# One last routing group of eight units, both limited experts fixed after 16 units, and another seam between a Mamba-2 scan and a switch layer

## The chip, the cores and the metric

The kernel runs on one core of a Trainium2 chip. A core has five engines with a queue of instructions each: PE (TensorE, matmuls), ACT (ScalarE), DVE (VectorE), POOL (GpSimd) and SP (SyncE, which here only issues DMAs). They run side by side and wait for each other through semaphores; within a queue the order is that of the program. The metric is device time in microseconds (us) of one execution.

## The reference, cut to what matters

Two blocks follow each other. The first is a Mamba-2 scan over 4 sequences of 768 tokens with 8 heads of 32 elements and a state of 16; it is computed in chunks, with a masked product inside a chunk and a carried state between chunks. The second is a top-1 mixture of experts: each of the 3072 tokens picks one of 8 experts, is multiplied by two matrices with a Relu between, and is scaled by its gate.

```python
M = CB * L                                     # (C B^T) times decays, causal, within a chunk
y_intra = np.einsum('bhij,bhjd->bhid', M, xc)
y_inter = np.einsum('bhin,bhnd->bhid', Cc, state) * decay_to_i[:, :, :, None]
y[:, :, sl] = y_intra + y_inter
state = decay_full[:, :, None, None] * state + np.sum(Bx, axis=2)
...
logits = x @ w_gate                            # x is y with the heads side by side: (3072, 256)
expert_idx = np.argmax(logits, axis=1)
for e in range(E):
    mask = expert_idx == e
    xe = x[mask]
    h = np.maximum(xe @ w1[e], 0.0)
    ye = h @ w2[e]
    out[mask] = gate_w[mask, None] * ye
```

## The kernel before, in words

**Attention.** A unit is 128 tokens of one sequence; there are 24 units, numbered by chunk and then by sequence. The main loop has 12 steps `d`, each with the two units 2d and 2d+1. The order of instructions is written out by hand (`manual_schedule`), so what stands first in the source stands first in each engine's queue. A step holds, on PE: `rows` of the step before (L343, turns y back so that tokens lie on partitions, with the gate logits as extra columns), `own` (L287, this step's own contribution to the state), `y_old` (L322, the part from the carried state), in some steps `rank`, then `y_own` (L330, 16 matmuls with the masked product M), then `scores` of the next step (L273). DVE masks the scores (`weigh`, L278, one operation per unit), takes the rows out of PSUM (`rows_out`, L352) and sums the logits (L362). ACT copies y out of PSUM (`turned`, L336), makes the new state (`state`, L307) and masked copies of C (L261). POOL scales x (`scaled_x`, L266), adds the faded old state (L313) and writes finished rows to their places in HBM (`place`, L412).

**Routing.** Units form groups (`RGS`). When a group's logits are there, `choose` marks each token's expert and `count` adds up the group. One step later `rank` works out on PE at which place of its expert each token goes, `ranked` takes that out (L401, L402), and `place` stores a unit's 128 rows with one indirect DMA from POOL to the buffer `x_hbm`. Each expert has a first part of 256 places (P1) and a second one of up to 192 (P2). Experts 0 and 1 are limited: after a given number of units `cut` moves the next free place up to 256, so that the first part is fixed and can be read before the last tokens are ranked. Places left empty were filled beforehand with rows that point to no token. Expert 0 is limited after 16 units, expert 1 after 20. Because a place may write anywhere in `x_hbm`, it waits for reads of `x_hbm` that stand before it, and a read waits for the places before it.

**Seam.** After step 11 the attention's PSUM banks are given to the experts: four banks H for the up-projection (where g was), two banks Y for the output projection (where y was). The rows of step 11 are turned, expert 0's rows (tile `xs`, token by token) are transposed by PE (L518) and copied by ACT (L519), and the last four units are chosen.

**Experts.** For each expert, `m_h` makes 8 slices of 128 hidden elements: two matmuls of PE (L557) and a Relu on ACT (L566) per slice. `m_y` makes the output (L592), scaled by the gate (L579) and stored by an indirect DMA of POOL (L570). `between(f)` is called after slice `f` and issues what else is due: ranking and placing of the last group, reads (`m_load`), loads of weights, and the transposes of the next expert's rows (`m_xT`: tile `xb`, read with 256-byte pieces so that DVE can transpose it in blocks of 32, L526) with its gates. The second parts run at the end, in pairs of experts, at a size rounded up to a multiple of 4 from 128 on (`SIZES`).

Of the kernel before, what the change touches and what calls it, by code (L numbers as in the profile page):

```python
# [20 lines left out]
CH = 128  # L21
# [5 lines left out]
RGS = [4, 4, 4, 4, 4, 4]  # L27
CUT = 4
# [19 lines left out]
def ssd_then_moe(ctx, tc, xs_in, ae_in, wgx, w_gate, w1, w2, gx, gb, gc, ga, out):  # L48
# [233 lines left out]
    def own(d):  # L282
        if d // NP == NC - 1:
            return
        for s in range(2):
            for q in range(4):
                nc.tensor.matmul(A_ps[32 * q:32 * q + 32, 64 * s:64 * s + 64],  # L287
                                 lhsT=st[2 * d + s]["B"][:, 32 * q:32 * q + 32],
                                 rhs=st[2 * d + s]["xp"][:, 64 * q:64 * q + 64], start=(s == 0), stop=True,
                                 skip_group_check=True)  # L290
# [42 lines left out]
    def turned(d, a=0, b=KT):  # L333
        if a == 0:
            sd[d]["yT"] = wk.tile([128, KT, 2 * CH], FP32, name="yT")
        nc.scalar.copy(out=sd[d]["yT"][:, a:b], in_=y_ps[:, a:b, 0:2 * CH])  # L336
# [4 lines left out]
    def rows(d):  # L341
        for t, s in [(t, s) for t in range(KT) for s in range(2)]:
            nc.tensor.matmul(r_ps[:, s, 256 * t:256 * t + 160], lhsT=sd[d]["yT"][:, t, CH * s:CH * s + CH],  # L343
                                 rhs=turn[:, t].rearrange("p e h -> p (e h)"), start=True, stop=True,
                                 skip_group_check=True)

    def rows_out(d):
        n = 2 * d
        g = grp[n]
        k = n - R0[g]  # L350
        for a, b, o in ((0, D, 0), (D, DE, DM)):
            nc.vector.tensor_tensor(  # L352
                out=rt[g][:, k:k + 2, o:o + KT * 4 * (b - a)].rearrange("p s (t e h) -> p s t e h", t=KT, h=4),
                in0=r_ps.rearrange("p s (t z) -> p s t z", t=KT)[:, :, :, 4 * a:4 * b].rearrange(
                    "p s t (e h) -> p s t e h", h=4),
                in1=bc(Er[:, n:n + 2].rearrange("p s (t h) -> p s t h", h=4)[:, :, :, None, :],
                       [128, 2, KT, b - a, 4]), op=ALU.mult)
# [62 lines left out]
    def counts(g):  # L420
        p = r_ps[:, 1, 460:460 + E]
        nc.tensor.matmul(p, lhsT=ones_bf, rhs=cnt[:, g], start=True, stop=True, skip_group_check=True)
        return p

    def cut(e):


        p = r_ps[:, 1, 460:460 + E]
        c = cnt[0:1, CUT + e, e:e + 1]
        nc.vector.tensor_scalar(out=less[:, e:e + 1], in0=p[0:1, e:e + 1], scalar1=-float(P1), scalar2=0.0, op0=ALU.add,  # L430
                                op1=ALU.min)
        nc.vector.tensor_tensor(out=c, in0=c, in1=less[:, e:e + 1], op=ALU.subtract)
        if e == 0:
            nc.vector.tensor_reduce(bad[:, 0:1], p[0:1, 0:2], axis=AX, op=ALU.min)

    def over():
        p = r_ps[:, 1, 460:460 + E + 1]
# [30 lines left out]
    def m_load(i):  # L468


        p, e = jobs[i]
        if i == 0:
            xs = mo.tile([128, 2, W], FP32, name="xs")
            nc.sync.dma_start(out=xs, in_=x_hbm[e * NR:e * NR + P1, :].rearrange("(t p) w -> p t w", p=128))
            ex[i]["xs"] = xs
            ex[i]["lt"] = xs[:, :, DM:W]
            return
        r0, n = e * NR + P1 * p, (P1, P2)[p]
        xb = mo.tile([128, P1 // 32 * 64], FP32, name="xb", bufs=4)
        for c in range(4):  # L480
            nc.sync.dma_start(out=xb[32 * c:32 * c + 32, 0:2 * n].rearrange("p (r z) -> p r z", z=64),
                              in_=x_hbm[r0:r0 + n, 64 * c:64 * c + 64].rearrange("(r j) z -> j r z", j=32))
        ex[i]["xb"] = xb[:, 0:2 * n].rearrange("p (r i k) -> p k r i", k=KT, i=32)
        lt = mo.tile([128, 2, MID], FP32, name="lt", bufs=7)[:, 0:2 - p]
        nc.sync.dma_start(out=lt, in_=x_hbm[r0:r0 + 128 * (2 - p), DM:W].rearrange("(t p) w -> p t w", p=128))
        ex[i]["lt"] = lt
        if p and e % 2 == 0:
            lh = mo.tile([128, 1, MID], FP32, name="lh", bufs=3)
            for u in range(2):
                q = r0 + u * NR + 128  # L490
                nc.sync.dma_start(out=lh[64 * u:64 * u + 64, 0], in_=x_hbm[q:q + 64, DM:W])
            ex[i]["lh"] = ex[i + 1]["lh"] = lh
# [18 lines left out]
    def m_xT0():  # L511

        ex[0]["xT"] = mo.tile([128, KT, P1], FP32, name="xT", bufs=4)
        for k in range(KT):
            q = h_next()[:, 0:P1]
            for t in range(2):
                xs = ex[0]["xs"][:, t, 0:DM].rearrange("p (i k) -> p i k", k=KT)
                nc.tensor.transpose(q[:, 128 * t:128 * t + 128], xs[:, :, k], ident)  # L518
            nc.scalar.copy(ex[0]["xT"][:, k], q)  # L519

    def m_xT(i):
# [5 lines left out]
        for j in range(i, i + 1 + p):  # L527
            ex[j]["g"] = gates(ex[j]["lt"], 2 - p)
        if p:
            ex[i]["gh"] = gates(ex[i]["lh"], 1)  # L530
# [187 lines left out]
    with tc.manual_schedule():  # L718
# [37 lines left out]
        for d in range(ND):  # L756
# [23 lines left out]
            if k >= 0:  # L780
                rows(k)
            own(d)
# [6 lines left out]
            e_cut = {9: 0, 11: 1}.get(d)  # L789
            if q is not None:  # L790
                rank(q)
                if e_cut is not None:
                    counts(CUT + e_cut)
# [5 lines left out]
            if d < ND - 1:  # L799
                for s in range(2):  # L800
                    y_own(d, s, range(NH))
                if d == 4:
                    turn_both(1)
                turned(d)
                if d == 4:
                    take_both(1)
            else:
                for t in range(KT):
                    for s in range(2):
                        y_own(d, s, range(4 * t, 4 * t + 4))  # L810
                for t in range(KT):
                    turned(d, t, t + 1)
# [4 lines left out]
            if q is not None:  # L817
                ranked(q)
                if e_cut is not None:
                    cut(e_cut)  # L820
                todo += list(range(R0[q], R0[q] + RGS[q]))
            if k >= 0:
                rows_out(k)
                if d == 4:
                    take_totals(1)
            if d == 0:
                route_consts()
            if k >= 0:
# [18 lines left out]
            if d == 11:  # L847
                weakest()
        att.close()
# [5 lines left out]
        while todo:  # L855
            place(todo.pop(0))
        for k in range(4):
            load_w(1, 1, k)
        m_load(1)
        rows(ND - 1)  # L860
        rows_out(ND - 1)
        logits_of(ND - 1)
        m_xT0()
        choose(LAST)
        count(LAST)
        ex[0]["g"] = gates(ex[0]["lt"], 2)
        for i in range(E):
            def between(f):
                if i == 0:
                    if f == 1:  # L870
# [5 lines left out]
                        for k in range(8):  # L876
                            load_w(2, *divmod(k, 4))
# [105 lines left out]
```

## Time and profile before

| | |
|---|---|
| three runs | 255.92, 257.65, 258.58 us; median 257.65 |
| profiled execution | 257.61 us, of which the span from first to last instruction is 255.9 us |
| mean granted PE clock | 0.992 |
| PE busy | 241.0 us, 94% of the span, 2020 matmuls recorded |
| DVE, ACT, POOL busy | 88.8, 88.9, 84.2 us (35%, 35%, 33%) |
| DMA | 39.75 MB, 155 GB/s on average |
| first matmul of the experts | 71.28 us after the start of the span |
| last output store of the experts issued | 251.72 us |

All other times below are microseconds from the start of the span. A busy time of PE contains matmuls whose ends are modelled; an engine's idle time is given with the one that released it. "SPq" and "POOLq" are queues that only issue DMAs.

### The profile page before, as it was taken

To read this page: it belongs to the slowest core of one execution; us is meant where nothing else is said; L and a number is where in the kernel's file an instruction comes from. 1 tells how busy PE (TensorE), PEld (TensorE's weight loads), DVE (VectorE), ACT (ScalarE), POOL (GpSimd) and SP (SyncE) were. 2 spreads that over 40 slices of the span, in tenths; PEclk is the share of its full clock that TensorE was granted. 3 is DMA by queue.
4 is the path that set the end of the run, shared out by engine and by line. 5 is a ranking of instruction groups with operands and counts; after the bars stand their busy time and mean duration, and the time that the engine had idled before them with its cause. 6 is when DMAs were issued, how large, how long until landed. Compare 5 with 4: busy or idle time off the path is not lost. (4 is left out here: it accounts for less than half of the span.)

```text
span 255.9 us, 5488 instructions
## 1 busy us (share of the span) xinstructions
PE 241.0 (94%) x2020; PEld 202.2 (79%) x2020; DVE 88.8 (35%) x278; ACT 88.9 (35%) x291; POOL 84.2 (33%) x149
## 2 busy tenths in 40 slices
PE   8899899875799999999999999999999999999992
PEld 5667677653678888888888888888998968989781
DVE  4799876846642050121101101113306004222000
ACT  4656657540133222324141413323250520523300
POOL 3465778873424500605050611030310201213031
PEclk9999999997999999999999999999999999999999
DMA  6999978525332499869595959555212100101001
GB/s 174 315 340 303 354 273 244 195 97 170 124 101 65 132 279 242 303 150 316 112 348 145 292 136 329 117 115 83 54 40 43 48 4 16 45 8 38 3 15 44
DMA packets 35319, 39.75 MB, mean 155 GB/s; under 512 B 20604, under 2 KB 22718, under 8 KB 35264
## 3 DMA queue, kind: packets, MB, share of 16 engines
q1 hardware_dynamic: 32272, 30.37, 41.7%
q0 software_dynamic: 2880, 8.66, 9.0%
q8 instruction: 27, 0.44, 0.7%
q14 instruction: 28, 0.23, 0.3%
q10 hardware_dynamic: 112, 0.05, 0.1%
HBM read 29.72 MB, written 9.86 MB: 155 GB/s over the span
## 5 line engine op out<-in xcount | busy, mean ns | idle before, releaser
L557 PE MATMUL h_ps<-xT,w 128*128 128x256 f32 (+3 forms) x512 | 90.5, 335 | 0.6 <-issue 0.4
L557 PEld LDWEIGHTS h_ps<-xT,w 128*128 128x128 f32 x512 | 80.6, 190 | 8.6 <-ACT hT L632 0.6
L592 PE MATMUL y_ps<-w,hT 128*128 128x256 f32 x384 | 85.0, 380 | 0.0
L592 PEld LDWEIGHTS y_ps<-w,hT 128*128 128x128 f32 x384 | 72.6, 190 | 10.5 <-issue 0.8
L570 POOL DMA_INDIRECT out_dram<-yo,lt x22 | 21.8, 989 | 58.1 <-DVE yo L577 31.1
L566 ACT ACTIVATE hT<-h_ps 128x256 f32<-128x256 f32 x64 | 24.1, 383 | 25.2 <-PE h_ps L557 17.4
L278 DVE TENSOR_TENSOR M<-g,mask 128x1024 f32<-128x1024 f32 x24 | 28.3, 1219 | 10.2 <-PE g L273 5.5
L412 POOL DMA_INDIRECT x_hbm<-rows,pos x24 | 23.8, 990 | 17.4 <-DVE t_sub L502 7.3
L632 ACT ACTIVATE hT<-h_ps 128x128 f32<-128x128 f32 (+2 forms) x64 | 17.9, 292 | 24.5 <-PE h_ps L557 20.4
L505 DVE TENSOR_REDUCE t_se<-t_sub 128x1 f32<-128x8 f32 (+1 forms) x20 | 3.3, 164 | 63.3 <-ACT t_sub L503 48.8
L526 DVE STREAM_TRANSPOSE xT<-xb 128x384 f32<-128x384 f32 (+1 forms) x15 | 9.2, 630 | 41.9 <-DMA xb<-x_hbm 38.7
L579 ACT ACTIVATE yo<-y_ps,t_gt 128x256 f32<-128x256 f32 x14 | 6.6, 474 | 40.6 <-PE y_ps L592 40.6
L412 POOL DMA_INDIRECT x_hbm<-zrows,rest x8 | 7.7, 961 | 39.3 <-DMA lt<-x_hbm 23.7
L330 PE MATMUL y<-M,xp 128*32 128x128 f32 x384 | 15.6, 285 | 4.4 <-DVE M L278 4.0
L343 PE MATMUL r<-turn,yT 128*128 128x160 f32 x96 | 16.2, 312 | 3.6 <-issue 2.0
L343 PEld LDWEIGHTS r<-turn,yT 128*128 128x128 f32 x96 | 13.3, 189 | 8.0 <-issue 4.2
L336 ACT COPY yT<-y 128x512 f32<-128x512 f32 (+1 forms) x13 | 7.1, 554 | 29.8 <-PE y L330 24.6
L330 PEld LDWEIGHTS y<-M,xp 128*32 128x32 f32 x384 | 10.3, 111 | 7.8 <-DVE M L278 2.8
L266 POOL TENSOR_TENSOR xp<-xs_n,Ei 128x256 f32<-128x256 f32 x23 | 13.7, 618 | 6.7 <-DVE last L241 3.6
L261 ACT ACTIVATE cm<-xs_n,par 128x128 f32<-128x128 f32 x46 | 15.0, 418 | 1.6 <-DMA xs_n<-in_xs_dram 1.5
L273 PE MATMUL g<-cm,xs_n 32*128 32x256 f32 x192 | 15.1, 433 | 0.0
L570 POOL DMA_INDIRECT out_dram<-yh,lh x4 | 3.9, 983 | 33.5 <-ACT yh L606 21.5
(122 smaller groups left out, 146.4 us busy)
## 6 DMA issues: line engine op xcount, KB each, us to landing
w<-in_w_dram SPq DMA_DIRECT2D x64, 256.0 KB
xs_n<-in_xs_dram SPq DMA_DIRECT2D x20, 320.0 KB
xb<-x_hbm SPq DMA_DIRECT2D x28, 64.0 KB
xb<-x_hbm SPq DMA_DIRECT2D x32, 48.0 KB
xs_n<-in_xs_dram SPq DMA_DIRECT2D x4, 192.0 KB
x_hbm<-zrows SPq DMA_DIRECT2D x1, 672.0 KB
lt<-x_hbm SPq DMA_DIRECT2D x7, 80.0 KB
xs_n<-in_xs_dram SPq DMA_DIRECT2D x4, 128.0 KB
```

The source lines that it names most:

```text
L261: nc.scalar.mul(t[:, u], st[n]["CT"], par[:, u:u + 1])
L266: eng.tensor_tensor(out=t, in0=st[n]["x"].rearrange("p (h d) -> p h d", d=D), in1=bc(Ei[:, n, :, None], [128, NH, D]), op=ALU.mult)
L273: nc.tensor.matmul(g_ps[:, q, n % 2], lhsT=st[n]["BT"][r], rhs=st[n]["cm"][r].rearrange("p u i -> p (u i)"), start=True, stop=True)
L278: nc.vector.tensor_tensor(out=t, in0=g_ps[:, :, n % 2].rearrange("p q (u i) -> p q u i", u=2), in1=bc(mask[:, None, None, :], [128, 4, 2, ...
L330: nc.tensor.matmul(y_ps[o:o + D, h // 4, CH * s:CH * s + CH], lhsT=st[n]["xp"][:, D * h:D * h + D], rhs=st[n]["M"][:, h], start=first, sto ...
L343: nc.tensor.matmul(r_ps[:, s, 256 * t:256 * t + 160], lhsT=sd[d]["yT"][:, t, CH * s:CH * s + CH], rhs=turn[:, t].rearrange("p e h -> p (e ...
L412: s_ = nc.gpsimd.indirect_dma_start(out=x_hbm[:, :], out_offset=bass.IndirectOffsetOnAxis(ap=at, axis=0), in_=row, in_offset=None)
L557: nc.tensor.matmul(p[:, 0:n], lhsT=w[:, c:c + 128], rhs=xT[:, t, 0:n], start=(t == 0), stop=(t == KT - 1))
L566: nc.scalar.activation(ex[i]["hT"][:, f, 0:n], q, func=ACT.Relu)
L570: return nc.gpsimd.indirect_dma_start(out=out[:, :], out_offset=bass.IndirectOffsetOnAxis(ap=tok, axis=0), in_=yo[:, :], in_offset=None, b ...
L592: nc.tensor.matmul(p, lhsT=ex[i]["hT"][:, f, 128 * t:128 * t + 128], rhs=w_sb[e][1][:, f * DM:f * DM + DM], start=(f == 0), stop=(f == FT ...
L632: nc.scalar.activation(ex[i + u]["hT"][:, f, 0:n], q, func=ACT.Relu)
```

## The change

- The last two groups of four units become one of eight, which is chosen after step 11 and ranked in slice 4 of expert 0 (before: units 16 to 19 were ranked in step 11, units 20 to 23 in slice 1).
- Experts 0 and 1 are both limited after 16 units, in step 9, by one `cut`. The scratch columns for the counts move from 460 to 492 in their bank, since ranking eight units takes 64 columns.
- `own` stands after `y_old` and `rank` from step 2 on. Its first matmul then doesn't open the bank's accumulation, which `y_old` has done.
- In step 11 `rows` of step 10 stands after `y_own`; `turned` is one copy; `rows` of step 11 goes to the two banks Y, one per unit, and `rows_out` takes it from there in four pieces.
- Expert 0's rows are read as `xb` like all the others' and transposed by DVE (`m_xT(0)`), before the rows of step 11 are taken out; the special read, PE's transposes and ACT's copies go. The reads for expert 1 are issued with those for expert 0, in step 10.
- Weights of expert 2 are loaded right after the attention instead of in expert 0.
- The gates of an expert's first part are made in slice 1 of the expert itself instead of after its transposes; `weakest` (a test for very weak decay) moves from step 11 to step 9.

```diff
-RGS = [4, 4, 4, 4, 4, 4]
+RGS = [4, 4, 4, 4, 8]
 def own(d):
...
-  rhs=st[2 * d + s]["xp"][:, 64 * q:64 * q + 64], start=(s == 0), stop=True,
+  rhs=st[2 * d + s]["xp"][:, 64 * q:64 * q + 64], start=(s == 0 and d < NP), stop=True,
-    def rows(d):
+    def rows(d, to=None):
         for t, s in [(t, s) for t in range(KT) for s in range(2)]:
-            nc.tensor.matmul(r_ps[:, s, 256 * t:256 * t + 160], ...
+            nc.tensor.matmul((to[s] if to else r_ps[:, s])[:, 256 * t:256 * t + 160], ...
-    def rows_out(d):
+    def rows_out(d, of=None):
...
+        for s, m, p in [(s, 1, v[:, None]) for s, v in enumerate(of)] if of else [(0, 2, r_ps)]:
+            for a, b, o in ((0, D, 0), (D, DE, DM)):
...
-    def cut(e):
+    def cut():
-        p = r_ps[:, 1, 460:460 + E]
-        c = cnt[0:1, CUT + e, e:e + 1]
+        p = r_ps[:, 1, 492:492 + E]
+        c = cnt[0:1, CUT, 0:2]
...
 def m_load(i):
-        if i == 0:
-            xs = mo.tile([128, 2, W], FP32, name="xs")
-            nc.sync.dma_start(out=xs, in_=x_hbm[e * NR:e * NR + P1, :].rearrange("(t p) w -> p t w", p=128))
...
-    def m_xT0():
...
 def m_xT(i):
-        for j in range(i, i + 1 + p):
-            ex[j]["g"] = gates(ex[j]["lt"], 2 - p)
         if p:
+            for j in range(i, i + 2):
+                ex[j]["g"] = gates(ex[j]["lt"], 1)
             ex[i]["gh"] = gates(ex[i]["lh"], 1)
 # the main loop, step d, k = d - 1
             if k >= 0:
-                rows(k)
-            own(d)
+                if d < ND - 1:
+                    rows(k)
+            if d < NP:
+                own(d)
...
             if q is not None:
                 rank(q)
-                if e_cut is not None:
-                    counts(CUT + e_cut)
+                if q == CUT - 1:
+                    counts(CUT)
+            if d >= NP:
+                own(d)
...
             if d == 10:
                 m_load(0)
-            if d == 11:
+                m_load(1)
+            if d == 9:
                 weakest()
+        rows(ND - 2)
         att.close()
...
-        while todo:
-            place(todo.pop(0))
-        for k in range(4):
-            load_w(1, 1, k)
-        m_load(1)
-        rows(ND - 1)
-        rows_out(ND - 1)
-        logits_of(ND - 1)
-        m_xT0()
+        for e, u in ((1, 1), (2, 0), (2, 1)):
+            for k in range(4):
+                load_w(e, u, k)
+        rows(ND - 1, Y)
+        rows_out(ND - 2)
+        logits_of(ND - 2)
+        m_xT(0)
+        rows_out(ND - 1, Y)
+        logits_of(ND - 1)
         choose(LAST)
         count(LAST)
-        ex[0]["g"] = gates(ex[0]["lt"], 2)
         for i in range(E):
             def between(f):
+                if f == 1:
+                    ex[i]["g"] = gates(ex[i]["lt"], 2)
                 if i == 0:
-                    if f == 1:
+                    if f == FT // 2:
                         rank(LAST)
                         ranked(LAST)
                         for k in range(R0[LAST], NU):
                             place(k)
                         m_load(2)
-                        for k in range(8):
-                            load_w(2, *divmod(k, 4))
                         m_load(3)
```

## The prediction

> **What bounds the kernel now.** I read the totals of the page first, then busy time by stretch of the span, then the order of instructions from 53 to 86 us with what each waited for. The page's chain that ended last holds only the closing store, so the order has to be followed by hand.
>
> ```profile
> 54.40:58.80 4.40, 1.95 (x24) 1.54 (x24) 0.00 (x1) 2.46 (x9) 3.94 (x7) 1.00 0.42 156
> 61.20:64.30 3.10, 3.00 (x33) 2.03 (x34) 1.62 (x7) 0.59 (x1) 0.23 (x2) 0.56 0.91 298
> 66.70:69.10 2.40, 0.87 (x29) 0.59 (x24) 2.00 (x9) 0.42 (x2) 1.63 (x3) 1.00 0.14 54
> 71.30:79.05 7.75, 7.70 (x39) 6.22 (x40) 3.10 (x14) 3.16 (x9) 0.98 (x3) 1.00 0.38 91
> 79.05:251.00 171.95, 171.69 (x931) 150.79 (x929) 33.06 (x154) 51.09 (x158) 39.03 (x50) 1.00 0.46 130
> ```
>
> Columns: the stretch, its length, then busy time of PE, PE's weight loads, DVE, ACT and POOL, granted clock, DMA share, GB/s. From 79.05 to 251.00, all the experts after the first up-projection, PE is busy 171.69 of 171.95 us. So the end moves with the moment at which that stream begins, unless the change tears a hole into it. The holes are all before: steps 9 to 11 of the attention and the seam to expert 0.
>
> ```profile
> 53.00 1.01 POOL L412 DMA_INDIRECT x_hbm<-rows,pos  x1 [0.88 <-DVE less L430]
> 53.19 1.15 PE L273 MATMUL g<-cm,xs_n 32*128 32x256 f32 x16
> 58.80 2.36 DVE L278 TENSOR_TENSOR M<-g,mask 128x1024 f32<-128x1024 f32 x2 [4.59 <-remote]
> 64.15 1.35 PE L343 MATMUL r<-turn,yT 128*128 128x160 f32 x8
> 66.39 1.19 PE L330 MATMUL y<-M,xp 128*32 128x128 f32 x32
> 67.25 1.01 POOL L412 DMA_INDIRECT x_hbm<-rows,pos  x1 [3.99 <-DVE less L430]
> 68.68 0.65 ACT L336 COPY yT<-y 128x256 f32<-128x256 f32 x2 [5.61 <-PE y L330]
> 69.11 1.35 PE L343 MATMUL r<-turn,yT 128*128 128x160 f32 x8 [1.53 <-ACT yT L336]
> 70.30 0.63 PE L518 MATMUL h_ps<-ident,xs 128*128 128x128 f32 x4
> 71.61 0.37 ACT L519 COPY xT<-h_ps 128x256 f32<-128x256 f32 x1 [0.37 <-PE h_ps L518]
> 77.42 0.71 DVE L526 STREAM_TRANSPOSE xT<-xb 128x512 f32<-128x512 f32 x1 [3.03 <-DMA xb<-x_hbm]
> 80.04 0.98 POOL L412 DMA_INDIRECT x_hbm<-rows,pos  x1 [7.32 <-DVE t_sub L502]
> 86.50 1.79 SPq L481 DMA_DIRECT2D xb<-x_hbm  x4
> 102.69 0.38 ACT L566 ACTIVATE hT<-h_ps 128x256 f32<-128x256 f32 x1 [0.48 <-PE h_ps L557]
> ```
>
> A line gives start, busy time, engine, source line, and in brackets the idle time before it. The seam is a chain: y_own of step 11 ends at 67.58 (66.39 + 1.19), the copy to yT begins only at 68.68, rows 69.11, four transposes 70.30, two copies, the first full up-projection after 72.0. The 1.1 us before the copy is odd: in steps 2 and 3 the same copy follows its matmuls within 0.1 us (18.29 to 18.36). Here a place (the indirect store at 67.25) runs until 68.26. At 53.00 four places begin back to back, the score matmuls end at 54.34, and DVE's masking of their result waits until 58.80. I read this as: while POOL issues places, a release by PE can arrive late.
>
> [...] after the hole from 57.67 to 60.17 the clock is 0.50 from 60.5 to 63.9. [...] here the fourth place ends at 57.80, and the read that needs it goes out at 59.54. [...] expert 0's rows will now come in 256 B pieces. For that I use the trace's own case, 73.74 to 77.42.
>
> **The change, part by part.** Times are on the axis of the profiled run (span 255.9, time 257.61, 1.7 around it; the median of the three runs is 257.65, so the same sum applies to it).
>
> *Routing.* Units 16 to 23 become one group, so ranking units 16 to 19 and the counting and limiting of expert 1 leave step 11, and their four places leave 67.25 to 72.05. Expert 1 is limited after 16 units instead of 20. Counting with the reference's inputs, it has 222 tokens by then, so 34 of its 256 places stay empty, and its second part grows from 87 to 121. Expert 0's is 126; the pair runs at the larger, rounded up to 128, in both kernels: nothing.
>
> *Own state moved, limits joined, the weak-decay test earlier.* Eight own matmuls change places with y_old and rank in steps 2 to 9; both orders stand before y_own, which waits for the mask product. Nothing on PE (0.43 us either way round). The test costs DVE 0.55 us (0.40 + 0.15) in step 9, behind the wait until 58.80: nothing while that cover lasts, 0.45 without it. I take the four places of steps 9 and 10 and their stall as unchanged.
>
> *Seam.* Scores of step 11 end at 64.22 as before. y_old runs to 64.9. M of the two units is ready at 65.5 and 66.66 (two operations of 1.2 us from 64.30), so y_own's second unit runs 66.7 to 67.25. No place runs, so the copy begins at about 67.4 and ends at 68.0 (0.59). PE meanwhile does rows of step 10, formerly done at 64.15 in the wait for M: 8 records at 0.135 spacing, 67.2 to 68.5; rows of step 11 follow into the two output banks to 69.8. PE's transposes (0.63) and two ACT copies go. Instead DVE makes xT: rows_out of step 10 from 68.6 (0.87), logits (0.29), transpose (0.71), which ends at 70.5. xb must be there by 69.8: its reads start at 59.54 as the old one did, land after 3.7 us by the later case, near 63.3, and expert 1's reads and twelve weight loads queue behind it, not before. So the up-projection starts at 70.55, limited by DVE, with PE idle some 0.8 us.
>
> *Expert 0.* Eight slices at 0.864 (7.07 over 32 records, spacing 0.216) are 6.91. Before, 71.28 to 79.05 is 7.77: 6.91, 0.58 for the second half of xT at 72.03, and some 0.3 for ranking. After, ranking needs ten small matmuls for six; estimate 0.6. The output projection starts at 70.55 + 6.91 + 0.6 = 78.06 instead of 79.05: **0.99 us earlier**. The exp of the gates stands behind DVE's longer row work (two 128x512-equivalents in four pieces, 1.2, plus choice and counts, to 73.5); it holds the third Relu to 74.2, and its bank is wanted after 75.5. PE's ranking waits for DVE's choice, made near 72.5, and PE is there at 74.9. From expert 1 on the gates are asked for in the expert's own slice 1 instead of the slice 4 before; DVE has their inputs by then, so their exp holds up no Relu: nothing.
>
> *Eight places in the expert stream.* Ranking comes in slice 4, near 74.9; positions at 75.9. The old last group waited until 80.04, although its positions were ready at 74.39: a place overwrites x_hbm and must wait for expert 1's reads, which now landed long ago. Eight at 1.27 run to 85.9, against 84.8 before. POOL's two stores of expert 0 stand behind them, 1.2 later; three yo buffers cover that. SP's reads for expert 2 go out near 87.6 instead of 86.5, land by 91.5, and are used at 98.9: over 6 us of room. Expert 2's weights no longer stand before expert 3's reads. Nothing.
>
> *Sum.* 257.61 - 0.99 = 256.6.
>
> **Rivals.**
> 1. *The stall at 54.4 to 58.8 changes.* Its cause is inferred, and the earlier ranking in steps 3 to 9 shifts places by up to 0.4 us. Without it masking would begin at about 54.9: 3.9 us, and 1.2 more if the half clock goes too; with the seam 6.1, so 251.5. For: the lag is irregular (1.8 us at 55.08, 4.4 at 58.80). Against: the four places and the instructions around them are the same.
> 2. *Late releases inside expert 0 (the slower side).* Eight places now run from slice 5 on. If a PE release waits for the bundle's end, as in step 10, the last Relus come at about 86.9 (85.9 + 0.97); the output projection needs slice 5 at 80.2: 6.7 us lost, 257.6 - 1.0 + 6.7 = 263.3. It decides once a Relu is over 2 us late. Against: four stores and places run from 102.62 to 107.45, and Relus stay on their 0.86 grid from 102.69; the old last group at 80.04 left the output copy at 82.70, 3.65 after its matmuls' start, as for the next expert (93.00 to 96.65).
> 3. *The seam is colder or xT later.* [...] half of 3.4 us is 1.7, so 258.3. Against: from 67.3 to 70.7 it is busy 1.86 of 3.40 now and keeps full clock. An xb that lands late costs the same kind of sum, one for one beyond 69.8.
>
> That the limits trigger the general path is excluded by 222, above the required 192.
>
> **How the numbers follow.** The forecast has 0.62, rival 1 0.12, rival 2 0.12, rival 3 0.14. The likeliest gives 256.6, and with the spread of the runs (255.9 to 258.6) and 1 us for the attention steps, 255 to 258. The range 253.8 to 259.8 takes in rival 3 and a part-size rival 1 and leaves out the ends of rivals 1 and 2. About 1% is what a measurement of this kernel can tell from no change: below 255.1 I put rival 1 and a tail of the forecast, 0.19; above 260.2 rival 2 and little else, 0.13; between, 0.68.
>
> **What would show it.** Right: no place between 58 and 75; the last yT copy at once after y_own; one 128x512 transpose on DVE near 69.8 and the up-projection following it; eight places from about 76; PE busy throughout from 78 on. Wrong: gaps of PE during the eight places, a masking of step 10 far from 58.8, half clock after 64, or DVE waiting for xb at the seam.

## The result: 1% slower on the first chip, 1% faster on three others

On the chip of the comparison on record the changed kernel takes 260.28 us (median of 9 executions, 258.47 to 262.19), the kernel before 257.65 (9 executions, 254.85 to 259.16). The ratio is 1.011, with a 95% interval of 1.0071 to 1.0149. The forecast was 256.6, its range 253.8 to 259.8: the time lies outside, on the other side. The experiments met other chips, named B to E here after A, the chip of the record, and on three of them the same two kernels stand the other way round:

| chip | before, us | changed, us | ratio (95% interval) |
|---|---|---|---|
| A | 257.65 | 260.28 | 1.011 (1.0071 to 1.0149) |
| C, first set | 251.07 | 248.44 | 0.988 (0.9839 to 0.9921) |
| D | 251.00 | 248.47 | 0.9911 (0.9885 to 0.9937) |
| C, second set | 250.86 | 248.46 | 0.9926 (0.9898 to 0.9954) |
| E | 250.95 | 248.75 | 0.9906 (0.9883 to 0.9929) |

Chip B, perhaps A again, is of A's sort (kernel before 256.72); the changed kernel itself was not run there. I call A and B "late" and C, D and E "in time", for a reason that the profiles give. Only C was met twice, so whether it is the chip or the visit that is late can't be told.

Times are medians of all executions, but ratios are taken from the fast runs alone, which on chip B leaves out those over 1.5% above the fastest of their kernel (20 of 47 of the kernel before, 9 of 20 of e3_four_later), so that a ratio there can differ from that of the medians by up to 0.6%.

### The profile page after: what moved, and what is told of

It is laid out like the page before. It is cut to its first block, busy times and chain, and to the rows that moved or that the text cites. A ratio compares the mean times of both kernels' runs of the same rounds, so it can differ in the third digit from the quotient of the medians.

```text
span 257.3 us, 5473 instructions
## 1 busy us (share of the span) xinstructions
PE 240.2 (93%) x2013; PEld 202.3 (79%) x2013; DVE 88.0 (34%) x274; ACT 87.7 (34%) x288; POOL 84.1 (33%) x147
## 5 line engine op out<-in xcount | busy, mean ns | idle before, releaser
L553 POOL DMA_INDIRECT out_dram<-yo,lt x24 | 23.8, 991 | 76.7 <-ACT yo L562 41.5
L331 PE MATMUL y<-M,xp 128*32 128x128 f32 x384 | 16.6, 292 | 4.7 <-DVE M L278 3.9
L331 PEld LDWEIGHTS y<-M,xp 128*32 128x32 f32 x384 | 11.4, 115 | 8.5 <-POOL xp L266 3.4
L336 ACT COPY yT<-y 128x512 f32<-128x512 f32 x12 | 7.0, 586 | 29.5 <-PE y L331 27.9
L343 PEld LDWEIGHTS r<-turn,yT 128*128 128x128 f32 x88 | 12.2, 189 | 5.5 <-ACT yT L336 3.9
L343 PE MATMUL r<-turn,yT 128*128 128x160 f32 x88 | 14.9, 312 | 1.7 <-ACT yT L336 1.1
L560 DVE TENSOR_SCALAR yo<-y_ps,t_gt 128x256 f32<-128x256 f32 x10 | 4.7, 484 | 23.9 <-PE y_ps L575 23.9
```

What stands on the lines that cost most here:

```text
L331: nc.tensor.matmul(y_ps[o:o + D, h // 4, CH * s:CH * s + CH], lhsT=st[n]["xp"][:, D * h:D * h + D], rhs=st[n]["M"][:, h], start=first, sto ...
L343: nc.tensor.matmul((to[s] if to else r_ps[:, s])[:, 256 * t:256 * t + 160], lhsT=sd[d]["yT"][:, t, CH * s:CH * s + CH], rhs=turn[:, t].rea ...
L553: return nc.gpsimd.indirect_dma_start(out=out[:, :], out_offset=bass.IndirectOffsetOnAxis(ap=tok, axis=0), in_=yo[:, :], in_offset=None, b ...
```

## The profile after

The profiled execution of the changed kernel took 259.0 us, its span is 257.3 (before: 257.61 and 255.9), so the profile shows 1.4 us of the 2.6 between the medians. Busy time by stretch, columns as in the prediction:

```profile
61.20:64.30 3.10, 3.05 (x36) 1.88 (x32) 1.09 (x4) 0.59 (x1) 0.00 (x0) 0.50 0.70 132
64.30:66.70 2.40, 2.02 (x36) 1.39 (x32) 2.17 (x2) 0.00 (x0) 0.00 (x0) 0.50 0.60 104
66.70:69.10 2.40, 2.26 (x35) 1.90 (x28) 0.29 (x2) 0.59 (x1) 0.00 (x0) 1.00 0.86 262
71.30:79.05 7.75, 7.75 (x45) 6.58 (x44) 4.10 (x18) 3.29 (x9) 2.33 (x6) 1.00 0.75 267
79.05:251.00 171.95, 169.46 (x923) 149.28 (x923) 31.71 (x150) 50.18 (x157) 41.27 (x55) 1.00 0.43 120
```

Two things are new: half clock (granted clock 0.50) lasts from 59.9 to 66.7, one stretch of 6.8 us, twice the 3.4 of the kernel before (60.5 to 63.9), and the expert stream has 2.5 us without PE (169.46 of 171.95 busy, before 171.69). The wait list of PE from 78 us on gives the place of that hole:

```profile
PE h_ps L540 <- ACT hT L549: 2.5, 1, 2.5
```

The timeline of the seam and of the hole:

```profile
58.86 2.36 DVE L278 TENSOR_TENSOR M<-g,mask 128x1024 f32<-128x1024 f32 x2 [4.08 <-remote]
64.53 2.36 DVE L278 TENSOR_TENSOR M<-g,mask 128x1024 f32<-128x1024 f32 x2 [2.20 <-PE g L273]
67.79 0.59 ACT L336 COPY yT<-y 128x512 f32<-128x512 f32 x1 [4.65 <-PE y L331]
70.88 4.58 PE L540 MATMUL h_ps<-xT,w 128*128 128x256 f32 x20 [0.83 <-DVE xT L509]
76.73 1.01 POOL L414 DMA_INDIRECT x_hbm<-rows,pos  x1 [3.56 <-DMA w<-in_w_dram]
...
85.35 3.62 PE L540 MATMUL h_ps<-xT,w 128*128 128x256 f32 x16
85.66 0.96 POOL L414 DMA_INDIRECT x_hbm<-rows,pos  x1 [0.21 <-issue]
86.78 0.47 ACT L562 ACTIVATE yo<-y_ps,t_gt 128x256 f32<-128x256 f32 x1 [4.20 <-PE h_ps L540]
86.92 1.00 POOL L553 DMA_INDIRECT out_dram<-yo,lt  x1 [0.30 <-issue]
88.23 1.00 POOL L553 DMA_INDIRECT out_dram<-yo,lt  x1 [0.30 <-issue]
91.03 0.66 ACT L549 ACTIVATE hT<-h_ps 128x256 f32<-128x256 f32 x2 [3.77 <-remote]
91.46 1.13 PE L540 MATMUL h_ps<-xT,w 128*128 128x256 f32 x4 [2.50 <-ACT hT L549]
```

PE makes four slices of expert 1 from 85.35 to 88.97. The first ended near 86.4, but ACT's first Relu comes at 91.03, and all four come in a bundle: PE's releases arrived late. The trace's records of PE's releases say the same, so it was not ACT that was late: four stand at 91.00, 91.06, 91.12 and 91.18. With its four PSUM banks full, PE stands until 91.46. GpSimd meanwhile had issued ten indirect DMAs without a break, eight places from 76.73 and expert 0's two stores at 86.92 and 88.23 (ended 89.23).

Profiled executions by milestones (start of the masking of steps 10 and 11, of the first and the last output projection, `m_y`), some of the experiments' too:

| kernel | step 10 | step 11 | first m_y | last m_y | last minus first |
|---|---|---|---|---|---|
| before | 58.80 | 64.30 | 79.05 | 243.75 | 164.70 |
| changed | 58.86 | 64.53 | 78.44 | 245.25 | 166.81 |
| e1_stores_later | 59.16 | 64.62 | 78.53 | 246.64 | 168.11 |
| e2_rank_early | 57.72 | 63.38 | 77.30 | 241.57 | 164.27 |
| e3_four_later | 55.49 | 59.78 | 73.69 | 238.25 | 164.56 |
| e4_two_groups | 59.50 | 65.17 | 78.97 | 243.23 | 164.26 |
| before, chip D (c1) | 52.60 | 57.70 | 71.07 | 237.12 | 166.05 |
| changed, chip D (c2) | 53.17 | 57.45 | 71.36 | 235.65 | 164.29 |
| changed, chip C (d1) | 52.36 | 56.63 | 70.69 | 235.06 | 164.37 |
| two groups, chip C (d4) | 52.48 | 57.69 | 72.89 | 237.43 | 164.54 |

For the first two rows the sum closes: +0.06 up to the masking of step 10, +0.17 to that of step 11 (its scores, made at half clock, take 2.09 us instead of 1.91), -0.84 from there to the first output projection (14.75 to 13.91, the new seam), +2.11 in the experts (the hole), -0.10 at the end: 1.40.

## The experiments

Theory: PE's releases are held up while GpSimd issues indirect DMAs back to back, and the row of ten tears the hole. First rival: the reads of expert 2's rows, issued at 88.31, do it. Second rival: the loss is the seam's longer half clock. The expectations call them A and B.

### Chip B, late: four variants of the changed kernel

**e1_stores_later**: expert 0's stores are issued after expert 1's up-projection.

```diff
-                put(p, ex[i]["lt"][:, t], ex[i]["g"][:, t:t + 1], i >= E - 1)
+                put(p, ex[i]["lt"][:, t], ex[i]["g"][:, t:t + 1], i >= E - 1, held if i == 0 else None)
...
             m_h(i, pp, between)
+            while i == 1 and held:
+                put_out(*held.pop(0))
```

> The changed kernel, with expert 0's two stores issued after expert 1's up-projection instead of at once behind the eight places. Theory (PE's releases are held up while GpSimd issues indirect DMAs back to back, ten of them from 76.7 to 89.2): the run is only eight and ends at 86.6, so the Relus of expert 1 come by about 87.5, PE's hole of 2.5 us in expert 1's up-projection shrinks below 0.5, time about 257.8. Rival A (the reads of expert 2's rows, 256 B pieces issued at 88.3, are what holds the releases): the hole stays 2.5 us, 260.3. Rival B (the loss comes from the seam and its longer half clock): no change, 260.3.

Measured: 260.05 us, ratio 1.0108 (1.0061 to 1.0154). The eight places alone leave no hole: expert 1's first Relu comes at 87.46, 1 us late, and the up-projection runs through. But the held stores now stand in another row, behind two stores of empty rows, and the hole is there. Timeline:

```profile
96.20 0.96 POOL L414 DMA_INDIRECT x_hbm<-zrows,rest  x1 [9.44 <-DMA w<-in_w_dram]
...
101.33 0.99 POOL L553 DMA_INDIRECT out_dram<-yo,lt  x1 [0.30 <-issue]
104.17 0.47 ACT L562 ACTIVATE yo<-y_ps,t_gt 128x256 f32<-128x256 f32 x1 [7.56 <-DMA out_dram<-yo,lt]
104.97 1.51 PE L540 MATMUL h_ps<-xT,w 128*128 128x256 f32 x3 [1.96 <-ACT hT L549]
```

Five in a row from 96.20 to 102.32; the output copy, due near 99.6, comes at 104.17, and PE stands for 1.96 us in expert 2. Behind it the granted clock is 0.64 from 104 to 108 and 0.93 from 108 to 112, which is worth 1.7 us at full clock, and the time stayed. The rival of the reads falls: those of expert 2's and 3's rows go out from 88.37 to 92.7, as in the changed kernel, and no hole follows; the next goes out at 103.83, 4 us after the new delay began. The exact form of the theory falls too: five did more harm than eight, and the kernel before had five in a row on chip A, from 80.04 to 86.12, with its copy on time:

```profile
85.12 1.00 POOL L570 DMA_INDIRECT out_dram<-yo,xs  x1 [0.30 <-issue]
86.15 0.47 ACT L579 ACTIVATE yo<-y_ps,t_gt 128x256 f32<-128x256 f32 x1 [2.98 <-PE y_ps L592]
```

So the length of a row does not decide by itself; what does stays open.

**e2_rank_early**: the last ranking in slice 2.

```diff
-                    if f == FT // 2:
+                    if f == 2:
                         rank(LAST)
```

> The changed kernel, with the last ranking in slice 2 of expert 0 instead of slice 4, so that the eight places start about 1.7 us earlier. Theory: the run ends 1.7 us earlier, near 87.5; the four late releases come near 89.3, the hole shrinks from 2.5 to about 0.8 us, time about 258.6. Rival A (reads): they too go out 1.7 us earlier, near 86.6, the same 0.8 us, so this run does not tell the two apart. Rival B (seam): 260.3.

Measured: 256.04 us, ratio 1.0035 (0.9997 to 1.0073), better than the 258.6 expected. No hole, where one of 0.8 us was expected; the releases are late all the same, but they arrive before PE has filled its four banks:

```profile
84.05 1.00 POOL L553 DMA_INDIRECT out_dram<-yo,lt  x1 [0.30 <-issue]
84.20 4.48 PE L540 MATMUL h_ps<-xT,w 128*128 128x256 f32 x20
86.71 0.47 ACT L562 ACTIVATE yo<-y_ps,t_gt 128x256 f32<-128x256 f32 x1 [5.29 <-PE h_ps L540]
87.08 0.65 ACT L549 ACTIVATE hT<-h_ps 128x256 f32<-128x256 f32 x2
```

Nine in a row end at 85.05, the copy due near 84.4 comes at 86.71, and the second store waits for it, which breaks the row.

**e3_four_later**: only four places in expert 0; the other four and the reads behind them in expert 1's slice 4.

```diff
-                        for k in range(R0[LAST], NU):
+                        for k in range(R0[LAST], NU - 4):
                             place(k)
-                        m_load(2)
-                        m_load(3)
...
                 if i == 1:
+                    for k in range(NU - 4, NU):
+                        place(k)
+                    m_load(2)
+                    m_load(3)
                     over()
```

> The changed kernel, with only four of the eight last places in expert 0 and four, with the reads of experts 2 and 3, in expert 1's slice 4. Theory: two runs of four and of two to four with a pause between them, as before the change; no hole at 88.97, time about 257.8, unless the later run, near 89 to 94, holds up expert 1's last releases. Rival A (reads): the reads move to about 94.5, so the hole would come near there, in expert 1's output projection, where only two releases are needed: about 258. Rival B (seam): 260.3.

Measured: 255.55 us, ratio 0.9901 (0.9869 to 0.9932), the only variant whose interval lies below 1 there; by the medians of all executions it is 0.9954 and e2_rank_early 0.9973. No hole. Its profiled execution also escaped more than half of the stall of step 10 (DVE waits 1.81 us instead of 4), although nothing ahead of the seam was changed:

```profile
53.27 0.96 POOL L414 DMA_INDIRECT x_hbm<-rows,pos  x1 [0.21 <-issue]
54.54 0.96 POOL L414 DMA_INDIRECT x_hbm<-rows,pos  x1 [0.22 <-issue]
55.49 2.35 DVE L278 TENSOR_TENSOR M<-g,mask 128x1024 f32<-128x1024 f32 x2 [1.81 <-PE r L343]
```

Here the masking runs at 55.49 amid the four places; in the other profiles of the late chips it comes 0.9 to 1.0 us after the last of them. So the stall varies between executions of the same instructions (1.81 us of waiting here, 4.02 in e2 on the same chip). The spread of the kernel before on this chip, 253.05 to 258.86 us, would fit. Part of e3's lead may be luck of this kind: 7 of its 20 executions took under 255 us, against 6 of 47 of the kernel before, and the medians of the rest are 256.29 and 256.82. The expectation for c4_four_later below names this rival; no run on a late chip tested it.

**e4_two_groups**: six groups of four again; both limits after 16 units and the new seam stay.

```diff
-RGS = [4, 4, 4, 4, 8]
+RGS = [4, 4, 4, 4, 4, 4]
...
+        while todo:
+            place(todo.pop(0))
         for e, u in ((1, 1), (2, 0), (2, 1)):
```

> The changed kernel with six routing groups of four again: units 16 to 19 are ranked and placed in step 11, units 20 to 23 in expert 0; both experts stay limited after 16 units and the new seam stays. Theory: four places in step 11 delay the copy to yT as before (about 0.9 us), four places and two stores in expert 0 leave no hole: 260.3 - 2.5 + 0.9 = 258.7, against 257.7 for the kernel before. Rival B (seam and half clock cost the time): 260 or more.

Measured: 256.98 us, ratio 1.0014 (0.9974 to 1.0055). No hole. The wait between masking and seam stayed (13.80 us from the masking of step 11 to the first output projection), since the step's places came only at 68.62, after the copy at 68.43; whether they would delay the copy was therefore not tested.

Together: the two profiles with a hole belong to the kernels at 1.011 and 1.0108, the three without to 0.990 to 1.0035. The rival of the seam falls as the main cause: all of these have the new seam, and it takes 13.80 to 13.92 us in all, in e3 too, whose mean granted clock was 1.000. Each of these kernels has one profile on a late chip (the changed one on A, the others on B), so that the hole goes with the time rests on five executions.

### Chip C, in time

> The changed kernel once more, for a second profiled execution and more times beside the same runs of the kernel before. Theory (a run of places and stores on GpSimd holds up PE's releases in expert 0 and 1): a hole of 2 us or more in an up-projection of expert 1 here too, and a time 2 to 4 us over that of the runs with the places split or earlier, about 260. Rival (the hole of the first profile was an accident of one execution, and the longer half clock of the seam is the cause): no hole, two windows of half clock, about 258.5.

Measured: 248.44 us, ratio 0.988; no hole. On this chip both the theory and its rival were wrong. **e6_spaced** puts a filling between the places:

```diff
+    gap = route.tile([1, 700], FP32, name="gap")
...
                             place(k)
+                            nc.gpsimd.memset(gap, 0.0)
```

> The changed kernel with a filling of a small unused tile by GpSimd (about 0.75 us) behind each of the eight places, so that they stand 2.1 us apart instead of 1.27; nothing else is moved. Theory that it is the lack of a break that builds up the delay: releases come in time, no hole in expert 1, about 257.5, although the stores of expert 0 now go out only near 93 and the reads of expert 2 near 93, landing near 97. Rival (the number of places ahead of the stores, or the stores themselves, decide): the hole stays, moved to where the stores go out, about 260.

Measured: 248.78, ratio 0.9896 (0.9855 to 0.9937); the places came 1.85 us apart. **e7_spread10** is e3_four_later with step 10 changed:

```diff
-            while todo and d == 10:
-                place(todo.pop(0))
             if todo:
-                place(todo.pop(0), False)
+                place(todo.pop(0), d >= 10)
+            if d == 11:
+                m_load(0)
+                m_load(1)
...
-            if d == 9:
-                for _ in range(2):
-                    place(todo.pop(0))
-            if d == 10:
-                m_load(0)
-                m_load(1)
+            if d in (9, 10):
+                place(todo.pop(0))
```

> The kernel with four of the last eight places in expert 1 (the one measured before), and in addition the four places that stood back to back at the start of step 10 taken apart: two before step 10's masking and two before step 11's, and the reads of expert 0's and 1's rows behind the last of them, in step 11. Theory: the stall of the masking of step 10 (4 us, 54.4 to 58.8) comes from the four back to back; with two and two it shrinks to about 1 us in each step, PE keeps full clock in most executions, about 253, against 255.5 without this edit. Rival (the stall has another cause): 255.5 and a masking of step 10 near 58 again. If the reads of the rows become late at the seam, up to 1 us is given back.

Measured: 250.02, ratio 0.996 (0.9939 to 0.9981). On this chip none of these tests its question: in all three the masking of step 10 stands near 52, and neither it nor an expert waits for a late release. The spread kernel pays 2.0 us of waiting for expert 0's late rows at the seam.

### Chip D, in time: both kernels profiled

> The kernel before, unchanged, for a profile on the chip of this call. Two chips have been seen: one on which PE's releases come late while GpSimd issues indirect DMAs (kernel before near 257), and one on which they do not (near 251). Theory: on a chip of the first kind the masking of step 10 comes near 58.8 again; on one of the second kind it comes within 1 us of the score matmuls, and PE waits neither there nor in experts 0 and 1, so that the time between the masking of step 11 and the output projection of expert 0 gives the price of the seam alone: 14.7 us, against 13.9 in the changed kernel.

> The changed kernel once more. Theory (the loss is late releases on chips that have them): near 260 with a hole of 2 us or more in expert 1 or 2 on a chip of the first kind, ratio about 1.01; near 248.5 without a hole on one of the second kind, ratio about 0.988. Rival (the seam's half clock decides): a hole or none, the ratio over 1.005 on every chip on which half clock follows the masking of step 10.

> The changed kernel with the eight places 2.1 us apart by fillings of an unused tile. On a chip with late releases: 257.5 if it is the lack of a break that builds up the delay, 260 if the number of places ahead of the stores or the stores themselves decide. On a chip without: 248.8 as before.

> The changed kernel with four of the eight last places, and the reads of experts 2 and 3, in expert 1's slice 4. Theory: it keeps the seam's gain and has no hole: about 0.99 of the kernel before on a chip with late releases (255.5 measured), and as fast as the changed kernel on one without (248.5); it would then be better than both kernels on both kinds of chip. Rival (its gain came from executions that happened to have no stall in step 10): 1.00 on a chip with late releases.

Measured: before 250.92 in its one execution (251.0 the median), changed 248.47 (0.9911), spaced 248.89 (0.9926, 0.9902 to 0.9949), four places later 248.61 (0.9923, 0.9897 to 0.995). The changed kernel's row of ten, in time:

```profile
78.27 4.48 PE L540 MATMUL h_ps<-xT,w 128*128 128x256 f32 x20
78.47 0.47 ACT L562 ACTIVATE yo<-y_ps,t_gt 128x256 f32<-128x256 f32 x1 [2.98 <-PE y_ps L575]
78.55 0.96 POOL L414 DMA_INDIRECT x_hbm<-rows,pos  x1 [0.23 <-issue]
79.82 1.00 POOL L553 DMA_INDIRECT out_dram<-yo,lt  x1 [0.30 <-ACT hT L549]
81.12 0.99 POOL L553 DMA_INDIRECT out_dram<-yo,lt  x1 [0.30 <-issue]
82.64 2.84 PE L540 MATMUL h_ps<-xT,w 128*128 128x256 f32 x12
```

The same ten, the same places in the stream, and the copy follows its matmuls at once. So a row of indirect DMAs is not enough; it takes a chip, or a visit, of the late sort.

Where does the changed kernel gain here? My expectation for c1 is wrong: from the masking of step 11 to the first output projection the kernel before needs 13.37 us, the changed one 13.91. Without late releases the old copy to yT came at 61.08, before the place at 62.93, and nothing was there to be saved. The gain lies elsewhere. The kernel before has a hole of its own in expert 1; its timeline:

```profile
82.66 1.84 SPq L481 DMA_DIRECT2D xb<-x_hbm  x4
86.67 0.71 DVE L526 STREAM_TRANSPOSE xT<-xb 128x512 f32<-128x512 f32 x1 [2.12 <-DMA xb<-x_hbm]
88.06 0.21 ACT L503 ACTIVATE t_sub<-t_sub 128x16 f32<-128x16 f32 x1 [5.18 <-DVE t_sub L502]
88.18 0.92 ACT L566 ACTIVATE hT<-h_ps 128x256 f32<-128x256 f32 x3
```

and its wait list:

```profile
PE y_ps L592 <- ACT hT L566: 1.3, 1, 1.3
```

In slice 4 of expert 1 the kernel asks for expert 2's gates. Their exp stands on ACT ahead of the Relus of slices 5 to 7 and waits for the rows' landing (86.6), so the Relus come at 88.18 and PE loses 1.26 us. On chip A the same read went out at 86.50, 3.8 us later, while PE's expert 1 began 8.0 us later (85.95 against 77.97). The exp held up the same three Relus, but PE, already in the output projection, reached none of their slices before they were done, and nothing was lost:

```profile
93.00 7.07 PE L592 MATMUL y_ps<-w,hT 128*128 128x256 f32 x32
93.96 0.22 ACT L503 ACTIVATE t_sub<-t_sub 128x16 f32<-128x16 f32 x1 [3.10 <-DVE t_sub L502]
94.08 0.91 ACT L566 ACTIVATE hT<-h_ps 128x256 f32<-128x256 f32 x3
```

The change asks for the gates in the expert's own slice 1, where no landing is waited for. In the two profiles of chip D the experts take 166.05 and 164.29 us from the first to the last output projection; 1.26 of these 1.76 us are the hole.

### Chip C again: the grouping by itself

> The changed kernel again, on the chip of this call. Theory: on a chip with late releases (kernel before near 257) 260 and a hole of PE of 2 us or more behind the eight places and two stores, or half clock for two windows; on one without (before near 251) 248.5.

> The changed kernel with the eight places 2.1 us apart. On a chip with late releases: 257.5 and no hole if the lack of a break builds up the delay, 260 if the stores or the number of places decide. On a chip without: 248.8.

> Four of the eight last places in expert 1, and the four places of step 10 taken apart into two and two. On a chip with late releases: the masking of step 10 within 2 us of its score matmuls and about 253 if the four back to back make the stall, 255.5 if not. On a chip without: 250, as measured, since the later reads of expert 0's rows hold up the seam by 1 us.

> The changed kernel with six routing groups of four again, and everything else of the change kept. On a chip with late releases: about 1.00 of the kernel before, as measured, below the changed kernel beside it. On a chip without, where no hole has to be avoided: the choosing for units 16 to 19 stands ahead of the masking of step 11 again (about 1.2 us on DVE), so 249.5 against 248.5 for the changed kernel, and 251 for the kernel before.

The edits are those shown. Measured: changed 248.46 (0.9926), spaced 248.75 (0.9929, 0.9905 to 0.9954), spread 249.92 (0.998, 0.9939 to 1.0021), two groups 249.84 (0.9965, 0.9946 to 0.9984). So the grouping is worth 1.4 us of the 2.4. PE, DVE and GpSimd in step 10, first with two groups:

```profile
55.54 1.15 PE L273 MATMUL g<-cm,xs_n 32*128 32x256 f32 x16
56.19 1.34 DVE L379 TENSOR_TENSOR oh_all<-l_all,mx 128x32 bf16<-128x32 f32 x1
56.43 0.47 POOL L314 TENSOR_TENSOR S<-S,fa 128x128 f32<-128x128 f32 x1
56.85 1.19 POOL L266 TENSOR_TENSOR xp<-xs_n,Ei 128x256 f32<-128x256 f32 x2
57.56 0.21 DVE L408 TENSOR_REDUCE cs<-oh_all 128x8 f32<-128x32 bf16 x1
57.69 2.34 DVE L278 TENSOR_TENSOR M<-g,mask 128x1024 f32<-128x1024 f32 x2
```

then the changed kernel:

```profile
55.42 1.15 PE L273 MATMUL g<-cm,xs_n 32*128 32x256 f32 x16
56.63 2.36 DVE L278 TENSOR_TENSOR M<-g,mask 128x1024 f32<-128x1024 f32 x2 [0.82 <-PE g L273]
```

Choosing for units 16 to 19 (1.34 us and its neighbours) stands ahead of the masking of step 11, which begins at 57.69 instead of 56.63 (0.94 us of it arise after the masking of step 10). Without that choosing the masking waits for PE. The operation that takes 1.34 us here took 0.19 in the profile before on chip A, where GpSimd had nothing to do in the same moment:

```profile
62.53 0.19 DVE L377 TENSOR_TENSOR oh_all<-l_all,mx 128x32 bf16<-128x32 f32 x1
```

In the changed kernel on chip A it took 0.19 at 18.66 with no work of GpSimd beside it, and 0.36, 0.40 and 0.26 at 27.44, 38.17 and 48.50, where GpSimd's scaling `xp` ran beside it for 0.30, 0.34 and 0.21 of these. That GpSimd's `S` and `xp` beside it (56.43 to 58.04) make the 1.34 too would fit; it was not tried. (The first output projection is 2.2 us later. Behind PE's longer wait the granted clock in that execution was 0.73 from 58 to 62 and 0.85 from 62 to 66, which is worth 1.7 us at full clock; it was the slowest of its kernel.)

### Chip E, in time

> The changed kernel again. Theory: where PE's releases come late (kernel before near 257), 260 and a hole of PE of about 2 us behind the eight places and two stores in most executions; where they do not (kernel before near 251), 248.5.

> The changed kernel with the eight places 1.85 us apart. Where PE's releases come late: 257.5 and no hole if the lack of a break builds up the delay, 260 if the stores or the number of places decide. Where they do not: 248.8.

> Four of the eight last places in expert 1, and the four of step 10 taken apart into two and two. Where PE's releases come late: the masking of step 10 within 2 us of its score matmuls and about 253 if the four back to back make the stall, 255.5 if not. Where they do not: 250.

Changed 248.75 (0.9906), spaced 248.44 (0.9898, 0.9874 to 0.9921), spread 251.85 (1.0011, 0.9972 to 1.005), near 2 us over what was expected. The spread kernel waits 1.9 us at the seam in the profiled execution, where the granted clock is 0.80 from 62 to 66 and 0.77 from 66 to 70.

**What stays open.** No late chip came again. That spacing the places would close the hole, and that the four places in step 10 make its stall, was not seen either way. On the chips in time the spread kernel shows no gain in step 10 (masking at 52.59 with two and two, 52.67 with four in a row, chip E). The changed kernel was profiled on a late chip once; the 1.2 us by which its median difference exceeds the 1.4 of the profile are not explained.

## Why the prediction was wrong

**Failed step: "Eight places in the expert stream", summed as "Nothing".** In its place the profile has a hole of 2.50 us, and the experts as a whole take 2.11 us longer. I costed when the places end, what waits for them and which buffers cover that. I did not cost what the row does to PE's releases, though I had read exactly that effect in step 10. It belongs to rival 2, which I gave 0.12 and argued down with the four stores and places at 102.62 to 107.45 during which Relus stayed on their grid. That evidence was one row of one length in one execution; e1 shows a row of five that did harm. Rival 2's own place and size were off too: it put the delay in slice 5 of expert 0 at 6.7 us. The releases inside expert 0 came in time, but for that of the last output copy (86.78 instead of near 85.5); the hole is in slice 4 of expert 1, 2.50 us, because PE first fills its four banks. Its other number held: a Relu more than 2 us late decides (here the first was 4.6 late and PE lost 2.50; in e2 it was 1.8 late and PE lost nothing).

**Seam: right on the late chip, and not elsewhere.** Forecast 0.99 us from the removal of the place ahead of the copy; measured 0.84 from masking to output projection, and within 0.01 us of 13.91 again in e1, e2, e3 and c2. The copy now begins 0.12 us after its matmuls (67.67 to 67.79), as forecast. The first output projection began at 78.44, not 78.06: 0.23 from the later masking of step 11, 0.15 in the seam. On chip D the old seam is 0.54 us shorter than the new one, since the copy was not late there. The gain I had priced is the removal of a delay that such chips do not have. There the seam can also be longer: 14.48 us in e5 and 14.53 in f1, where the transpose waits some 0.5 us for expert 0's rows, the second half of rival 3.

**Rival 3 in part.** Half clock lasted 6.8 us instead of 3.4, as it feared, but cost only 0.17 us up to the masking of step 11 and nothing that shows in the seam (13.91, as in e3 at full clock), not 1.7, the estimate from half of the 3.4 us: PE was not the bound in those microseconds (at 65.90 it still waited 0.38 us for DVE's M).

**Routing: "Nothing" was wrong in its premise.** I saw only ranking and counting leave step 11. The choosing that leaves step 10 lets the masking of step 11 begin 0.94 us sooner after that of step 10 (d1 against d4). In the profile I had, that was covered: DVE waited 1.34 us for scores made at half clock. In d4, where the scores took 1.15 us instead of 1.91, DVE was the bound.

**Gates in the expert's own slice 1: "nothing".** I checked that no Relu would be held up in the new order, not whether one was held up in the old. Three were, on both chips; on chip A it cost nothing, on chip D 1.26 us.

**Rival 1** had the right sense of where the time varies (the stall of step 10 is much shorter in e3's profile and absent on every chip in time), but it is not the change that moves it.

The safest of the versions measured is four places in each of the two experts: 0.9901 of the kernel before on chip B (0.9954 by all medians, part of it perhaps luck) and 0.9923 on chip D, where the changed kernel beside it had 0.9911, no difference. On the late chips it stands against the changed kernel only through the kernel before (0.990 on B, 1.011 on A).

## What to carry to other kernels

A profile shows one chip: stalls that come from late releases, and covers that depend on them, may be absent on the next one (in the kernel before, the masking of step 10 waited 4.59 us on chip A, not at all on chip D), so cost a change both with and without the stall. When work is moved into a full stream, ask not only who waits for it but what its engine's activity does to the releases of others (up to 4.6 us of delay here). Splitting a row of indirect DMAs of GpSimd took the hole of 2.50 us away in e3 and e4; that mere breaks inside the row would do was not seen. When a step leaves an engine, list what stood behind it on that engine, also where the profile shows that engine idle.

## What the hardware showed unasked

- On chips A and B PE's releases came up to 4.6 us late around rows of indirect DMAs of GpSimd; on C, D and E they came at once behind the same rows (c2: Relus 0.86 to 1.00 us apart from 81.92 to 85.51, the row's end at 82.11), and the same program, the kernel before, took 251 instead of 257 us. Where they were late they mostly came 0.8 to 1.9 us after the row's end (57.80 to 58.80, 86.68 to 87.46 in e1, 85.05 to 86.71, 89.23 to 91.03, 102.32 to 104.17), in a bundle.
- The traces of chip A also lack records of PE's releases: 280 stand for 295 releases issued in the changed kernel, 272 for 298 in the kernel before. Other engines' records are fewer too (ACT, kernel before: 228 on chip A, 272 on chip D). Whether that has to do with the late releases was not shown, and whether releases would be late in an execution without a trace was not tried.
